# Four PSUM banks instead of two for the later pairs' scores and applications, in a newly found static order

## The chip, the cores and the metric

The kernel runs on one core of one Trainium2 chip. The metric is the time of one execution on the device in microseconds, the median of several runs. The engines are TensorE (PE in the rows), VectorE (DVE), ScalarE (ACT), GpSimd (POOL) and SyncE (SP, which issues the transfers). Each engine works through its own instructions in the order in which the program issues them.

## The reference

Three layers follow one another. The first is attention with 2 batches of 8 heads, 768 rows and 64 columns. Each row attends to the keys less than 16 rows away, and besides to one summary of each block of 32 rows: the maximum of its keys and the mean of its values.

```python
k_sum = k.reshape(B, H, nb, block, D).max(axis=3)
v_sum = v.reshape(B, H, nb, block, D).mean(axis=3)
scores_l = scale * np.matmul(q, k.transpose(0, 1, 3, 2))
scores_s = scale * np.einsum('bhsd,bhnd->bhsn', q, k_sum) + np.log(block)
scores_all = np.concatenate([np.where(mask_l, scores_l, -1e9), scores_s], axis=-1)
a = np.exp(scores_all - np.max(scores_all, axis=-1, keepdims=True))
x = np.matmul(a / (np.sum(a, axis=-1, keepdims=True) + 1e-09), np.concatenate([v, v_sum], axis=2))
```

The heads' outputs are joined to x, 1536 tokens of 512. The second layer divides x by its root mean square, multiplies it by a gain, and computes `silu(xn @ w_gate) * (xn @ w_val) @ w_out` with 1536 inner columns. The third computes `elu(x @ w_in) @ w_out` with 2048 inner columns.

## The kernel before

All three layers are fused and stay in the core's SBUF as far as they can. The 24 tiles of 64 query rows are handled as twelve pairs (b, j): batch b, pair j of 0 to 5. The 1536 tokens form three blocks of 512; the first block is made by the pairs (0,0) to (0,3). Matrix products are computed as three products of high and low parts of the operands (`THREE`), so each weight chunk and each x is split into a rounded copy (a cast, mostly ScalarE, L135) and the rest (a subtraction on VectorE, L146). The weights arrive in a packed form which `convert_a`, `convert_l` and `convert_b` turn into floats (L258 to L278) before the split.

For one pair `add_pair` lists these steps:

- `scores` (L495) writes 32 small matmuls into two PSUM banks, one for each half of the heads.
- `add_mask` on VectorE (L502) adds the mask and takes the maximum, `exps` on ScalarE (L513) takes the exponentials and their sums, and `normalize` divides (L528, L530, L533).
- `turn_e` (L538) transposes the weights on TensorE, one bank for each half; `copy_e` copies them out.
- `apply_v2` (L550) multiplies them with the values, one bank, and `copy_x2` copies the result to x, `xT`.

Around them stand `max_k` (L334, VectorE: the block maxima of the keys, `ksum`), `mean_v` (L370, TensorE: the sums of the values, `vp`), and for the first block the root mean square in two halves of 256 tokens: `square` and `add_square` (L635 to L641), `sum_square` (L648, TensorE, into a bank `pss`), `mean_square` (L653, VectorE), `root` (L659, POOL), `diagonal` (L672), `spread` (L686, TensorE), `keep_root`. `x_hi` and `x_lo` (L735, L744) split x times the gain.

The first feed-forward layer's products are `project` (L764): `pg` is a gate projection of one weight chunk, `pv_..c` the value projection, and the down products `acc` stand in L820. The blocks 1 and 2 later go through products of sums of quarter matrices (L1001, L1179).

PSUM has eight banks, each held by one tile at a time. A tile that takes a bank waits until its last holder's readers are done.

```python
MM, AT, ACC = ("m0", "m1"), ("t0", "t1"), ("a0", "a1", "a2", "a3")
BANKS = AT + MM + ACC[::-1]
```

The first four pairs may use all of `BANKS`; the eight later pairs, beside which the feed-forward layers already run, use `AT` for scores, transposes and applications, while the projections take `MM` and the down products `ACC`.

What sets the order is written out by hand as two tables. `PLAN` lists 2835 codes: a code divided by four is the operation's number, the rest is the choice among the engines that may do it. `TAGS` lists, digit by digit, which bank of its tuple a tile takes. The costs and due times in `add` are read by nothing while the kernel runs.

```python
for code in PLAN:
    i, choice = divmod(code, 4)
    engine, _, _, fn, args, _, _, new = self.ops[i]
    for tag, name in new:
        self.tag_of[name] = tag[int(next(picks))] if isinstance(tag, tuple) else tag
    fn(*((list(engine)[choice],) if isinstance(engine, dict) else ()), *args)
```

## Time and profile before

| | |
|---|---|
| median of 3 runs | 579.91 us (579.61 to 580.13) |
| profiled execution | 580.1 us, its span 578.4 us |
| granted clock of TensorE | 1.000 |
| busy: TensorE, VectorE, ScalarE, POOL | 571.3, 545.4, 428.3, 31.2 us |

The span goes from the first to the last instruction; what lies around it is 1.7 us here. Busy time of TensorE is that of its matmuls, whose ends are modelled, so rows of its timeline overlap: how long a step takes is read there from its start to the start of the next one. In a timeline, `x6` means six instructions of one form in a row, and a bracket at a row's end gives the idle time before it and what ended it.

### The profile page before, as it was taken

The page shows a single profiled execution, that of the slowest core. Times are in us where ns is not written, and L with a number is a line of the kernel's source. Part 1 is how long each engine was busy: PE and PEld are TensorE (multiplying, and loading weights), DVE is VectorE, ACT ScalarE, POOL GpSimd, SP SyncE. Part 2 cuts the span into 40 slices and gives each one's busy share as a digit, 9 for nine tenths or more (in the row PEclk, how much of TensorE's full clock was granted, in tenths as well). Part 3 has the DMA queues.
Part 4 walks back from the last instruction along what each step waited for, and adds up shares of the span by engine and source line. Part 5 has one row for each costly group of instructions (what it writes and reads, how often), then busy time and mean ns, then how long its engine had stood idle before and what let it go on. Part 6 is the DMA issues. An engine that isn't in the chain of part 4 may idle for free.

```text
span 578.4 us, 10028 instructions
## 1 busy us (share of the span) xinstructions
PE 571.3 (99%) x3369; PEld 467.6 (81%) x3369; DVE 545.4 (94%) x1155; ACT 428.3 (74%) x954; POOL 31.2 (5%) x73
## 2 busy tenths in 40 slices
PE   9899999999999999999999999999999999999997
PEld 5688787888878888888888888888888888888886
DVE  6999999999989999998799999999999999999992
ACT  5999997989999987643445557586577798879741
POOL 5630200000000000000000000000000000000000
PEclk9999999999999999999999999999999999999999
DMA  8999999889579994225251117242356527065112
GB/s 315 311 331 331 350 335 334 304 275 344 197 265 347 298 352 187 65 68 158 92 161 57 39 44 228 66 136 65 100 163 202 170 96 217 11 196 156 23 49 106
DMA packets 56181, 109.06 MB, mean 189 GB/s; under 512 B 6785, under 2 KB 19585, under 8 KB 56129
## 3 DMA queue, kind: packets, MB, share of 16 engines
q1 hardware_dynamic: 56128, 108.42, 56.6%
q8 instruction: 26, 0.43, 0.3%
q14 instruction: 27, 0.21, 0.1%
HBM read 80.09 MB, written 28.31 MB: 187 GB/s over the span
## 4 chain that ended last, share of the span: by engine, by line
PE 86%; DVE 9%; ACT 2%; issue 1%; DMA 1%; POOL 1%; SPq 0%; ACTq 0%; POOLq 0%
PE acc L820 12%; PE B_1u L1001 8%; PE ph L764 8%; PE A_1u L1001 6%; PE C_1u L1001 6%; PE B_2u L1001 6%; PE B_2d L1179 6%; PE B_1d L1179 4%; PE C_2d L1179 4%; PE C_2u L1001 4%; PE A_2u L1001 4%; PE A_2d L1179 4%; PE C_1d L1179 3%; PE A_1d L1179 3%; PE pg L764 2%; PE pv L550 2%
## 5 line engine op out<-in xcount | busy, mean ns | idle before, releaser
L1001 PE MATMUL B_1u<-xh,w_1u 128*128 128x512 f32 x144 | 48.4, 390 | 0.0
L764 PE MATMUL ph<-xa,ws_i 128*128 128x512 f32 x192 | 46.0, 392 | 0.0
L764 PEld LDWEIGHTS ph<-xa,ws_i 128*128 128x128 f32 x192 | 35.7, 188 | 7.6 <-issue 0.2
L764 PE MATMUL pg<-xs,ws_g 128*128 128x512 f32 (+1 forms) x168 | 36.4, 364 | 0.0
L1179 PE MATMUL B_2d<-td,wd 128*128 128x512 f32 x144 | 35.1, 389 | 0.0
L135 ACT CAST wd<-rd 128x512 fp32r<-128x512 f32 x49 | 29.7, 619 | 5.2 <-PE B_1d L1179 2.5
L146 DVE TENSOR_TENSOR wd<-rd,wd 128x512 fp32r<-128x512 f32 x49 | 32.7, 686 | 0.0
L1001 PE MATMUL C_1u<-xh,w_1u 128*128 128x512 f32 x96 | 32.6, 389 | 0.0
L1001 PE MATMUL B_2u<-xh,w_2u 128*128 128x512 f32 x96 | 32.6, 389 | 0.0
L1001 PE MATMUL A_1u<-xh,w_1u 128*128 128x512 f32 x96 | 32.5, 389 | 0.0
L1001 PEld LDWEIGHTS B_1u<-xh,w_1u 128*128 128x128 f32 x144 | 27.0, 188 | 6.0 <-ACT B_1u L135 0.3
L764 PEld LDWEIGHTS pg<-xs,ws_g 128*128 128x128 f32 x168 | 27.9, 189 | 4.6 <-issue 0.2
L1179 PEld LDWEIGHTS B_2d<-td,wd 128*128 128x128 f32 x144 | 27.0, 188 | 5.6
L1001 PE MATMUL B_1u<-xl,w_1u 128*128 128x512 f32 x72 | 28.0, 389 | 0.0
L135 ACT COPY h_1u<-B_1u 128x512 f32<-128x512 f32 x19 | 11.1, 590 | 22.6 <-PE B_1u L1001 19.7
L1179 PE MATMUL B_1d<-td,wd 128*128 128x512 f32 x108 | 26.5, 391 | 0.0
L1179 PE MATMUL C_2d<-td,wd 128*128 128x512 f32 x96 | 25.0, 389 | 0.0
L513 ACT ACTIVATE e<-e,nm 128x120 f32<-128x120 f32 x64 | 24.4, 387 | 0.0
L135 ACT CAST td<-z 128x512 fp32r<-128x512 f32 x28 | 17.1, 618 | 9.8 <-DVE z L1162 7.2
L1179 PEld LDWEIGHTS B_1d<-td,wd 128*128 128x128 f32 x108 | 20.2, 188 | 4.5 <-ACT B_1d L135 0.3
L1179 PE MATMUL A_2d<-td,wd 128*128 128x512 f32 x93 | 23.5, 389 | 0.0
L1001 PE MATMUL C_2u<-xh,w_2u 128*128 128x512 f32 x64 | 21.8, 389 | 0.0
(545 smaller groups left out, 1743.9 us busy)
## 6 DMA issues: line engine op xcount, KB each, us to landing
st_i<-in_moe_w_in SPq DMA_DIRECT2D x16, 512.0 KB, 5.7
st_p<-in_moe_w_out SPq DMA_DIRECT2D x16, 512.0 KB, 6.0
st_g<-in_moe_w_gate SPq DMA_DIRECT2D x12, 512.0 KB, 6.3
st_v<-in_moe_w_val SPq DMA_DIRECT2D x12, 512.0 KB, 5.9
st_o<-in_moe_w_out SPq DMA_DIRECT2D x12, 512.0 KB, 5.6
kept_i<-raw_i SPq DMA_DIRECT2D x16, 256.0 KB, 5.6
kept_p<-raw_p SPq DMA_DIRECT2D x16, 256.0 KB, 5.1
va<-in_v SPq DMA_DIRECT2D x17, 192.0 KB, 5.4
```

The source lines that it names most:

```text
L135: nc.scalar.copy(out=out, in_=in_)
L146: (nc.gpsimd if eng == POOL else nc.vector).tensor_sub(out, a, b)
L513: nc.scalar.activation(out=e[:, pr, :], in_=s[:, pr, :], func=AF.Exp, bias=nm[:, pr:pr + 1], scale=1.0 if pre else -1.0, accum_out=ss[:, p ...
L550: nc.tensor.matmul(pv[64 * h:64 * h + 64, pr, n, :], va[:NK, 2 * pr + h, :], T[f"ats{b}_{j}_{h}"][:, pr, QT * n:QT * n + QT], start=True, ...
L764: nc.tensor.matmul(pt[:, i], wt[:, a, kk * P:(kk + 1) * P], xt[:, c, i], start=(kk == 0 and n == 0), stop=(kk == KM - 1 and n == 2))
L820: nc.tensor.matmul(acc, wt[:, a, cs], ot[e], start=(first and n == 0), stop=(last and n == 2))
L1001: nc.tensor.matmul(pt, wt[:, a, cs], xt[e][:, kk], start=first and kk == n == 0, stop=kk == 1 and n == 2, skip_group_check=not first)
L1179: nc.tensor.matmul(pt, wt[:, a, cs], xt[:, e], start=first and n == 0, stop=last and n == 2, skip_group_check=i not in (0, 5))
```

## The change

Scores and applications of the eight later pairs may now use the banks of the projections too: `wide` is `AT + MM` for them, and a digit of `TAGS` chooses among four. Transposes stay in `AT`. Three costs in `add` are smaller. With these, the search that makes the two tables was run anew: the first 26 codes and the last 1363 of `PLAN` are the old ones, those between are another order. Every operation of the old table stands in the new one. Some 75 operations have another engine; in the lists of instructions ScalarE has 9 rows more than before, VectorE 5 and POOL 3 fewer. Lines behind L569 are one higher in the changed kernel.

```diff
     def add_pair(b, j, due, tags):
         i = b * NQ + 2 * j
         early = i < TPB
+        wide = tags if early else AT + MM
...
-            add(PE, 1.0, due + 0.5, scores, b, j, tags, pre, r=[f"q{b}_{j}"] + kas, w=[f"s{n}" for n in ns],
+            add(PE, 0.97, due + 0.5, scores, b, j, wide, pre, r=[f"q{b}_{j}"] + kas, w=[f"s{n}" for n in ns],
...
-                new=[x for n in ns if not pre for x in (("e", f"e{n}"), (tags, f"s{n}"))])
+                new=[x for n in ns if not pre for x in (("e", f"e{n}"), (wide, f"s{n}"))])
...
-            add(PE, 0.48, at + 5.2, turn_e, b, f"{j}_{h}", tags, r=[f"e{n}"], w=[f"at{n}"], new=[(tags, f"at{n}")])
+            add(PE, 0.465, at + 5.2, turn_e, b, f"{j}_{h}", tags, r=[f"e{n}"], w=[f"at{n}"], new=[(tags, f"at{n}")])
...
-        add(PE, 1.14, due + 6.9, apply_v2, b, j, tags, r=[f"ats{x}" for x in ns] + [x + y for x in bufs for y in ("#a", "#s")],
+        add(PE, 1.10, due + 6.9, apply_v2, b, j, wide, r=[f"ats{x}" for x in ns] + [x + y for x in bufs for y in ("#a", "#s")],
-            w=[f"pv{b}_{j}"], new=[(tags, f"pv{b}_{j}")])
+            w=[f"pv{b}_{j}"], new=[(wide, f"pv{b}_{j}")])
...
-    40, 48, 52, 80, 320, 64, 60, 212, 226, 84, 229, 218, 108, 232, 236, 92, 584, 112, 96, 336, 480, 120, 340, 326,
+    20, 40, 48, 52, 80, 320, 64, 60, 212, 226, 84, 229, 218, 108, 232, 236, 92, 584, 112, 96, 336, 480, 120, 340, 326,
...
-    "2551001014507341614711001241075617267054601543015125100101101010001101010010110001010011010011010101"
+    "2551001014507341614711001241075617267056314250320115010010111021011000231010101221001110110030010120"
```

On TensorE the first 37 and the last 300 operations are in their old order (from 24.9 to about 305 us they differ), on VectorE the first 35 and the last 480. What stands at three places follows, as lists of instructions without times; a name ends in the tile's number, and `x3` stands for three in a row.

VectorE, before, where the first pairs end (`ats` are transposed weights copied out, `rs` a reciprocal, `raw_v` and `raw_g` weight chunks being converted):

```order
L137 COPY xT_171<-pv_0_541 128x4x128
L523 RECIPROCAL rs_3_0_587<-ss_3_0_563 128x4
L137 COPY ats_2_1_632<-at_2_1_591 120x512
L523 RECIPROCAL rs_3_1_634<-ss_3_1_569 128x4
L269 TENSOR_SCALAR raw_v_662<-st_v_583 128x512
L530 TENSOR_TENSOR e_3_1_568<-e_3_1_568,rs_3_1_634 128x480
L278 SCALAR_TENSOR_TENSOR raw_v_662<-st_v_583,raw_v_662 128x512
L274 SCALAR_TENSOR_TENSOR raw_g_667<-st_g_581 128x512
L641 TENSOR_TENSOR 0, 1)slice(0, 256, None)_676<-0, 1)slice(0, 256, None)_676,2, 3)slice(0, 256, None)_678 128x512
```

And of the change:

```order
L334 TENSOR_REDUCE ksum_197<-kT_1_580 128x4x4
L137 COPY ats_1_0_583<-at_1_0_533 120x512
L137 COPY xT_171<-pv_0_542 128x4x128
L523 RECIPROCAL rs_3_0_591<-ss_3_0_564 128x4
L523 RECIPROCAL rs_3_1_645<-ss_3_1_570 128x4
L137 COPY ats_2_1_647<-at_2_1_596 120x512
L269 TENSOR_SCALAR raw_v_652<-st_v_587 128x512
L530 TENSOR_TENSOR e_3_1_569<-e_3_1_569,rs_3_1_645 128x480
L274 SCALAR_TENSOR_TENSOR raw_g_607<-st_g_585 128x512
L334 TENSOR_REDUCE ksum_197<-kT_2_626 128x4x4
L278 SCALAR_TENSOR_TENSOR raw_v_652<-st_v_587,raw_v_652 128x512
L642 TENSOR_TENSOR 0, 1)slice(0, 256, None)_633<-0, 1)slice(0, 256, None)_633,2, 3)slice(0, 256, None)_631 128x512
```

Two block maxima of the second batch (`ksum_197`, from `kT_1` and `kT_2`) now stand here. Before, they stand some 50 rows further down or more.

VectorE, before, where the first products' operands are made (`xs_0` to `xs_3` are the parts of x, `ws_v` and `ws_g` weight chunks; `ws_g_760` is gate chunk 0, `ws_g_766` gate chunk 2):

```order
L744 SCALAR_TENSOR_TENSOR xs_3_721<-xT_171,g_sb,xs_3_721 128x256
L274 SCALAR_TENSOR_TENSOR raw_g_730<-st_g_598 128x512
L744 SCALAR_TENSOR_TENSOR xs_2_719<-xT_171,g_sb,xs_2_719 128x256
L146 TENSOR_TENSOR ws_v_754<-raw_v_662,ws_v_754 128x512
L744 SCALAR_TENSOR_TENSOR xs_1_758<-xT_171,g_sb,xs_1_758 128x256
L744 SCALAR_TENSOR_TENSOR xs_0_717<-xT_171,g_sb,xs_0_717 128x256
L146 TENSOR_TENSOR ws_g_760<-raw_g_667,ws_g_760 128x512
L146 TENSOR_TENSOR ws_g_766<-raw_g_730,ws_g_766 128x512
```

And of the change, where `ws_g_756` is chunk 0 and `ws_g_814` is chunk 2:

```order
L146 TENSOR_TENSOR ws_g_756<-raw_g_607,ws_g_756 128x512
L274 SCALAR_TENSOR_TENSOR raw_g_784<-st_g_603 128x512
L143 TENSOR_SCALAR xs_0_683<-xT_171,g_sb 128x256
L143 TENSOR_SCALAR xs_3_687<-xT_171,g_sb 128x256
L745 SCALAR_TENSOR_TENSOR xs_0_683<-xT_171,g_sb,xs_0_683 128x256
L745 SCALAR_TENSOR_TENSOR xs_1_738<-xT_171,g_sb,xs_1_738 128x256
L745 SCALAR_TENSOR_TENSOR xs_2_685<-xT_171,g_sb,xs_2_685 128x256
L745 SCALAR_TENSOR_TENSOR xs_3_687<-xT_171,g_sb,xs_3_687 128x256
L638 TENSOR_TENSOR  1)slice(256, 512, None)_867<-xT_171 128x512
L146 TENSOR_TENSOR ws_g_814<-raw_g_784,ws_g_814 128x512
```

Between the splits of chunks 0 and 2 there are now the conversion of chunk 2, two `x_hi`, the second half's four `x_lo` and a square.

TensorE, before, at the first products (`pss` is the first half's sum of squares, `s_5` the scores of pair (0,5), `pv_3` an application):

```order
L648 MATMUL pss0slice(0, 256, None)_710<-ones,0, 1)slice(0, 256, None)_676 128x4 x4
L495 MATMUL s_5_0_732<-ka_10_379,q_5_600 64x120
...
L550 MATMUL pv_3_771<-ats_3_0_752,va_168 64x64
...
L764 MATMUL pv_0c<-xs_0_717,ws_v_754 128x256 x3
...
L764 MATMUL pg_0_816<-xs_0_717,ws_g_760 128x256 x3
...
L764 MATMUL pg_2_854<-xs_0_717,ws_g_766 128x512 x3
L764 MATMUL pg_2_854<-xs_1_758,ws_g_766 128x512 x3
L648 MATMUL ss0slice(256, 512, None)_861<-ones, 1)slice(256, 512, None)_839 128x4 x4
```

And of the change:

```order
L649 MATMUL pss0slice(0, 256, None)_742<-ones,0, 1)slice(0, 256, None)_633 128x4 x4
L550 MATMUL pv_3_759<-ats_3_0_754,va_168 64x64
...
L495 MATMUL s_5_0_788<-ka_10_380,q_5_605 64x120
...
L765 MATMUL pv_0c<-xs_0_683,ws_v_740 128x256 x3
...
L765 MATMUL pg_0_842<-xs_0_683,ws_g_756 128x256 x3
...
L765 MATMUL pg_0_842<-xs_0_683,ws_g_756 128x256 x3
...
L765 MATMUL pg_2_888<-xs_0_683,ws_g_814 128x512 x3
L765 MATMUL pg_2_888<-xs_1_738,ws_g_814 128x512 x3
L649 MATMUL ss0slice(256, 512, None)_895<-ones, 1)slice(256, 512, None)_867 128x4 x4
```

The scores of (0,5) have moved behind application (0,3), and gate chunk 0 is finished in both halves (`pg_0_842` twice four instructions) ahead of chunk 2.

TensorE, before, at the scores of pair (1,0) (`s_0_0` and `s_0_1`) and the application of (0,4) (`pv_4_1316`):

```order
L764 MATMUL pv_4c<-xs_1_758,ws_v_1136 128x512 x3
L495 MATMUL s_0_0_1248<-ka_0_1227,q_0_1166 64x120
L495 MATMUL s_0_1_1249<-ka_0_1227,q_0_1166 64x120
...
L764 MATMUL pv_4c<-xs_2_719,ws_v_1136 128x512 x3
L764 MATMUL pv_4c<-xs_3_721,ws_v_1136 128x512 x3
L820 MATMUL acc_0_0_1286<-act_0_0h,ws_o_1174 128x512
...
L550 MATMUL pv_4_1316<-ats_4_0_1235,va_170 64x64
L550 MATMUL pv_4_1316<-ats_4_1_1162,va_170 64x64
```

And of the change:

```order
L765 MATMUL pv_4c<-xs_3_687,ws_v_1117 128x512 x3
L495 MATMUL s_0_0_1269<-ka_0_1239,q_0_970 64x120
L495 MATMUL s_0_1_1270<-ka_0_1239,q_0_970 64x120
...
L495 MATMUL s_0_1_1270<-ka_1_1166,q_0_970 64x120
L550 MATMUL pv_4_1289<-ats_4_0_1252,va_170 64x64
L550 MATMUL pv_4_1289<-ats_4_1_1248,va_170 64x64
...
L550 MATMUL pv_4_1289<-ats_4_1_1248,va_230 64x64
L765 MATMUL pg_6_1337<-xs_0_683,ws_g_1100 128x512 x3
```

Six matmuls of a value projection and six of the down products stood between the two steps; now the application is right behind the scores.

## Rows read from the trace of the kernel before

**Rows 1.** The page: busy time of each engine, share of the span, instructions.

```profile
PE 571.3 (99%) x3369; PEld 467.6 (81%) x3369; DVE 545.4 (94%) x1155; ACT 428.3 (74%) x954; POOL 31.2 (5%) x73
```

**Rows 2.** The list of TensorE's waits: us in total, times, longest us.

```profile
PE at L538 <- POOL e L528: 1.4, 2, 0.7
```

**Rows 3.** Windows, the stretch from 22 to 57 us: busy time of each engine.

```profile
22.00:57.00 35.00, 34.32 (x388) 30.09 (x386) 34.38 (x99) 34.49 (x93) 10.78 (x15) 1.00 0.93 314
```

**Rows 4.** TensorE's timeline, 127 to 138 us: start, us, what, count [idle before].

```profile
127.20 1.52 PE L764 MATMUL pv_10c<-xs,ws_v 128*128 128x512 f32 x6
128.65 1.05 PE L495 MATMUL s<-ka,q 64*64 64x120 f32 x32
129.63 1.67 PE L764 MATMUL pv_10c<-xs,ws_v 128*128 128x512 f32 x6
131.14 0.39 PE L820 MATMUL acc<-act_7h,ws_o 128*128 128x512 f32 x1
...
135.24 1.52 PE L764 MATMUL pg<-xs,ws_g 128*128 128x512 f32 x6
136.60 1.52 PE L764 MATMUL pv_11c<-xs,ws_v 128*128 128x512 f32 x6
```

**Rows 5.** TensorE's timeline, an application between products.

```profile
149.88 1.15 PE L550 MATMUL pv<-ats,va 120*64 120x64 f32 x32
150.96 0.50 PE L820 MATMUL acc<-act_11h,ws_o 128*128 128x512 f32 x1
151.29 0.39 PE L820 MATMUL acc<-act_11l,ws_o 128*128 128x512 f32 x1
```

**Rows 6.** TensorE's timeline, transposes and an application, 94 to 100 us.

```profile
94.23 0.60 PE L538 MATMUL at<-ident,e 128*120 128x128 f32 x4
94.58 1.63 PE L764 MATMUL pv_7c<-xs,ws_v 128*128 128x512 f32 x6
96.06 0.60 PE L538 MATMUL at<-ident,e 128*120 128x128 f32 x4
96.58 1.15 PE L550 MATMUL pv<-ats,va 120*64 120x64 f32 x32
...
98.93 0.40 PE L820 MATMUL acc<-act_3h,ws_o 128*128 128x512 f32 x1
99.52 0.65 PE L538 MATMUL at<-ident,e 128*120 128x128 f32 x4 [0.19 <-DVE xT L137]
```

**Rows 7.** TensorE's timeline, the early stretch.

```profile
29.43 1.16 PE L495 MATMUL s<-ka,q 64*64 64x120 f32 x32 [0.28 <-PE 0slice(0, 256, None)_710 L648]
30.52 0.92 PE L550 MATMUL pv<-ats,va 120*64 120x64 f32 x24
...
32.10 1.69 PE L764 MATMUL pv_0c<-xs,ws_v 128*128 128x256 f32 x12
...
36.45 1.04 PE L648 MATMUL lice(256, 512, None)_861<-ones,lice(256, 512, None)_839 128*128 128x4 f32 x8
...
42.37 1.75 PE L764 MATMUL pg<-xs,ws_g 128*128 128x512 f32 x6
```

**Rows 8.** VectorE's timeline, the same stretch.

```profile
29.25 0.47 DVE L744 SCALAR_TENSOR_TENSOR xs<-xT,g_sb,xs 128x256 fp32r<-128x256 f32 x1
...
33.25 0.27 DVE L502 CUSTOM_DVE_ANT_0 e<-s,mask 128x120 f32<-128x120 f32 x1
...
34.13 1.66 DVE L744 SCALAR_TENSOR_TENSOR xs<-xT,g_sb,xs 128x256 fp32r<-128x256 f32 x4
35.71 0.68 DVE L641 TENSOR_TENSOR lice(256, 512, None)_839<-lice(256, 512, None)_839,lice(256, 512, None)_835 128x512 f32<-128x512 f32 x1
36.31 0.67 DVE L334 TENSOR_REDUCE ksum<-kT 128x16 f32<-128x512 f32 x1
```

**Rows 9.** POOL's timeline, the two roots of the first block.

```profile
34.28 0.90 POOL L659 TENSOR_TENSOR 0slice(0, 256, None)_841<-0slice(0, 256, None)_810,mhalf 128x2 f32<-128x2 f32 x1 [0.16 <-DVE 0slice(0, 256, None)_810 L653]
38.86 2.04 POOL L659 TENSOR_TENSOR lice(256, 512, None)_894<-lice(256, 512, None)_885,mhalf 128x2 f32<-128x2 f32 x1 [3.67 <-DVE lice(256, 512, None)_885 L653]
```

More of the change, by code (lines that the diff above doesn't have):

```diff
@@ L1353 @@
     392, 152, 357, 296, 301, 264, 396, 176, 156, 164, 172, 180, 360, 592, 365, 185, 520, 116, 268, 124, 492, 497, 525,
[146 rows of a table removed]
[146 rows of a table added]
 )
 TAGS = (
-    "2551001014507341614711001241075617267054601543015125100101101010001101010010110001010011010011010101"
-    "0010101010110100100110110012222011032111012200416700322510242117120215102402217620102321100604512120"
+    "2551001014507341614711001241075617267056314250320115010010111021011000231010101221001110110030010120"
+    "0110101010110100101101100100011122003122001012560004230721420200110701251412217620102321100604512120"
     "1212631050101032047120100112140022625222010213122640172000115222002600010530111047231562102072202130"
```

292 rows, old and new, of the table PLAN are left out of this document.

## The prediction

> **What bounds the kernel now.** I read the page first. TensorE is busy 571.3 us of a span of 578.4 [rows 1], at the full granted clock, so the time is close to the sum of the matmuls, which the change leaves as they are. Only three things can move: time in which TensorE waits, time lost where it goes from one kind of matmul to another, and new waits.
>
> The list of TensorE's waits comes next [rows 2]. It holds very little, 3.4 us in six rows: its largest is 1.4 us for POOL's normalization of the first pairs, ahead of 24.9 us, where the order on TensorE stays as it is, and of the others only waits of 0.2 to 0.3 each lie where the order changes [rows 6, 7]. The windows then say which engines have no room while the attention and the first feed-forward block run side by side: from 22 to 57 us VectorE is busy 34.38 of 35 us and ScalarE 34.49 [rows 3]. There, whatever is put ahead of an urgent instruction on these two engines makes that one later by about its own length. Behind 57 us there is more room on both, and TensorE has only one short wait there that the change touches.
>
> Last I read TensorE's timeline from start to start, because the ends of its matmuls are modelled and the rows overlap.
>
> **Joins.** Six products alone take 1.36 us (135.24 to 136.60). The six ahead of a scores step take 1.45 (127.20 to 128.65), the scores 0.98 (128.65 to 129.63), the six behind them 1.51 (129.63 to 131.14) [rows 4]. Going into scores so costs 0.09 and going back to products 0.15. An application takes 1.08 (149.88 to 150.96), and the one product behind it 0.33 where one alone takes 0.23 (a sixth of 1.36), so its way back costs 0.10 [rows 5]; its way in I take as that of scores, 0.09.
>
> With four banks to choose from, later scores can now stand right beside an application: scores of pair (1,0) and application (0,4), application (0,5) and scores (1,1), application (1,1) and scores (1,2). None of the old order's later steps has such a join. Each saves one way back and one way in. Scores first: 0.15 + 0.09 = 0.24, less what going from scores to an application costs. One early row shows at most 0.11 for that: the scores at 29.43 last 1.09 until the application at 30.52, against 0.98 [rows 7]. Application first: 0.10 + 0.09 = 0.19, less a change that no row shows, 0 to 0.11. I take the row's 0.11 for the first join, which leaves 0.13, and nothing for the change of the other two, since no row shows one: 0.13 + 2 x 0.19 = 0.51. The bounds are 0.13 + 2 x 0.08 = 0.29 and 0.24 + 2 x 0.19 = 0.62. The Trainium skill, page TensorEngine Tiling (Array Packing), section Key Properties, says that a change of tiling mode, not merely of the tile, drains TensorE. Scores stand in the trace as 64*64 and applications as 120*64, so by that page a join would still hold one drain of the four; as an estimate from it the three joins would give 3 x 0.43 / 4 = 0.32 (0.43 is the sum of the four costs above), and the forecast would be 0.2 us higher. The early row at 29.43 agrees with it, with its 0.11, and is a single one.
>
> Transposes of the weights (`turn_e`) have four joins more than before. A row of that kind exists: a transpose at 96.06, then an application at 96.58, 0.52 together with the change. Alone the transpose takes 0.35 (94.23 to 94.58), its way back 0.12 (the six products from 94.58 to 96.06 take 1.48), and the way into an application 0.09: 0.56 [rows 6]. The gain is 0.04 a join, and I cost it at nothing.
>
> **The wait at 99.** The product at 98.93 is followed by the next transpose only at 99.52, 0.59 instead of 0.23 [rows 6]: the transpose (1,1,0) goes into the bank t0 that application (1,0) holds until it is copied out. In the changed order that application goes into m0, and both transposes stand ahead of it. The 0.36 goes.
>
> **The gate projection at 42.** Six products from 42.37 last 1.75 where 1.52 is usual [rows 4, 7]; this is 0.2 of waiting for the split of weight chunk 3. The changed order puts the value sums (24 short matmuls) ahead of it, which hide it: 0.2 gained.
>
> **The early stretch.** Here VectorE's order matters, and it is the largest term. Three edits are behind it. Two block maxima of the second batch (`max_k`) stood at 36.31 and at 44.63 and now stand before the first masks of pair (0,4); a row of 0.67 or 0.68 takes 0.60 from start to start (35.71 to 36.31), so everything behind them comes 1.2 later [rows 8]. The sums of squares of the first half go to bank t0, which the scores of pair (0,5) need next, so these wait for `mean_square` on VectorE. And the split of gate chunk 2 moves behind the second half's x work, while TensorE now asks for it after 24 half products of chunk 0 instead of 12.
>
> First the scores: the masks of (0,4) end at about 29.3 in the trace; 1.2 for the maxima, 0.6 for the split of the value chunk and 0.4 for one `x_lo` (a quarter of 34.13 to 35.71) give 31.45, `mean_square` 0.07 more. The scores start at 31.5, last 0.98, and the first products start at 32.5 instead of 32.10 [rows 7, 8]: 0.38 lost.
>
> Then chunk 2: its split ends by 33.25 now. Ahead of it come the two maxima 1.2, four `x_lo` 1.58, one square 0.6, and two `x_hi` on VectorE, which the trace doesn't have at this width; the nearest row is an `x_lo` of the same shape at 0.40, and a plain scaling with one input less can't be far under half of that, so 0.3 each, bounds 0.2 and 0.4. The sum is 3.98, and the split ends at 37.23 [rows 8]. TensorE is there after the same amount of work as from 32.10 to 36.45, so at 32.48 + 4.35 = 36.83 [rows 7]. It waits 0.4. The lag behind the old order is 37.23 - 36.45 = 0.78, which holds the 0.38. Bounds: nothing, if one of the two inputs comes earlier by another engine's work, and 1.2, if the maxima's full price reaches TensorE. Other moved work (about 75 operations change their engine, some 5 us more for ScalarE) lies from 57 us on beside products that don't wait for it; I cost it at nothing, and a few tenths if that cover fails.
>
> One load is moved: the second batch's keys (512 KB) go to SP's queue ahead of the first gate weights. Behind it on that queue are four loads that the first products need. No wait of TensorE is put down to a load in the list of waits, so these have room, and I cost the move at nothing; what it costs if the room is too small is one more delay of the first products, inside the bounds of the lag above.
>
> The sum is -0.51 - 0.36 - 0.2 + 0.78 = -0.3, and a tenth or two for a spread of the second half that comes late (below): -0.15. The profiled execution took 580.1 us, 0.2 over the median of the runs, 579.91, so the forecast is 579.8 on the median's scale.
>
> **Rivals.** A measurement of this kernel can tell about 0.2%, 1.16 us, from no change; that is the band of "same", 578.75 to 581.07.
>
> *Nothing is lost early.* If VectorE has more room than its busy time says, the early lag isn't there, and with it goes the 0.28 that the scores waited at 29.43 [rows 7]. Then -0.51 - 0.36 - 0.2 - 0.3 = -1.4, about 578.5; with the upper price for the joins and 0.04 for each of the transposes' four, 578.3. For it: the three old waits there are short and each has another cause. Against: the three edits on VectorE add up in rows, and nothing in them is free. Chance 0.27.
>
> *ScalarE stands behind the root.* The second half's `diagonal` moves from VectorE to ScalarE, and stands there ahead of the casts of gate chunk 3 and value chunk 1. Its input comes from POOL's power, which took 0.90 us once and 2.04 the other time [rows 9]. The second sums of squares come 2.2 later than now (37.23 + 1.42 for the chunk's first half, 38.65 against 36.45 [rows 7]); with the root 2.4 behind them as now (38.86), it starts at 41.1 and ends at 42.0 or at 43.1. If ScalarE is at the diagonal when the root starts, it stands idle for the root's length, in a stretch where it has 0.5 us of room in 35 [rows 3], and VectorE's splits behind its casts, then TensorE, get what is over. It decides when ScalarE stands there for more than about a us, half of which its room and TensorE's lag of 0.8 take up; the price is 1.2 to 2.0 on top of the sum, the upper end being a whole slow root, 581 to 581.8. The Trainium skill, page SBUF — State Buffer, section on two separate sides, says that VectorE and GpSimd share one pair of ports as an exclusive lock and that the loser fully blocks; a busy VectorE would by that make the slow root the usual one. The two rows of the root agree with that no more than with chance. The slower outcome has 0.21.
>
> *The change doesn't do what it says.* If a join costs as much as two separate entries, only the waits at 42 and 99 are gained: -0.56 + 0.78 + 0.15 = +0.4, 580.3. This lies in the same band.
>
> **How the numbers follow.** The likeliest case, with the last rival, is no measurable change: 0.52, at 579.8, its own range 579.1 (joins at 0.62, a lag of 0.4) to 580.9 (joins at 0.29, a lag of 1.2, the late spread and half a us of lost cover). Faster has 0.27 and slower 0.21 from the two others. The range takes in most of both: 578.2, just under the end of the first, to 581.8, the end of the second.
>
> **What would show it.** In the new trace: the three joins start to start (an application right behind scores at 1.0 to 1.1 us); no gap ahead of the transposes of (1,1); the first products near 32.5 and a gap of 0.4 ahead of gate chunk 2 near 37; ScalarE's idle time ahead of `diagonal`, with POOL as the releaser. The prediction is wrong if TensorE is ahead of its old self at equal work at 45 us, or more than 1.5 us behind it, or if new gaps of over half a us come up between 57 and 240 us.

## The result, and the profile after

The changed kernel took 587.15 us (median of 5 runs, 586.22 to 587.6); the kernel before took 580.13 beside it (579.61 to 581.15). The ratio is 1.0113, 95% interval 1.0102 to 1.0125: slower by 1.1%, outside the range of the prediction. The profiled execution took 586.43 us, its span 584.7, at a mean granted clock of 0.993. All five runs of the changed kernel lie at 0.993 or 0.994; the profiled execution of before has 1.000.

The page's busy times after, which answer to [rows 1]:

```profile
PE 573.8 (98%) x3369; PEld 470.8 (81%) x3369; DVE 544.5 (93%) x1148; ACT 432.9 (74%) x967; POOL 28.2 (5%) x70
```

The same matmuls, 2.5 us more of busy time, and 3.8 us more in which TensorE isn't busy (10.9 of 584.7 against 7.1 of 578.4). The list of TensorE's waits after, beside [rows 2]:

```profile
PE s L495 <- POOL ka L450: 2.7, 1, 2.7
PE at L538 <- POOL e L528: 1.4, 2, 0.7
...
PE pv L550 <- DVE ats L137: 0.8, 2, 0.6
PE pv L550 <- DMA va<-in_v: 0.5, 1, 0.5
PE pv L550 <- ACT ats L135: 0.3, 1, 0.3
```

The first row is new and is the largest: scores wait 2.7 us for POOL to fill a part of a key tile, `ka`. The windows show where, beside [rows 3] (start and end; busy us and instructions of PE, PEld, DVE, ACT, POOL; granted clock, DMA share, GB/s):

```profile
22.00:32.00 10.00, 8.56 (x166) 6.93 (x164) 9.96 (x33) 9.97 (x29) 6.39 (x8) 1.00 0.97 280
32.00:42.00 10.00, 7.32 (x67) 6.72 (x63) 8.77 (x29) 9.15 (x28) 2.87 (x3) 0.66 0.86 334
42.00:57.00 15.00, 15.00 (x137) 13.33 (x136) 11.26 (x28) 9.96 (x26) 0.99 (x2) 1.00 0.65 210
```

From 32 to 42 us TensorE is busy 7.32 us and its clock is granted at 0.66 of full speed: it stands still, and then it runs slowly. Behind 42 the other engines have room that they didn't have before. TensorE's timeline after, beside [rows 7]:

```profile
24.37 1.15 PE L550 MATMUL pv<-ats,va 120*64 120x64 f32 x32 [0.59 <-DVE ats L137]
...
28.37 1.15 PE L550 MATMUL pv<-ats,va 120*64 120x64 f32 x32 [0.26 <-ACT ats L135]
29.62 1.05 PE L649 MATMUL 0slice(0, 256, None)_742<-ones,)slice(0, 256, None)_633 128*128 128x4 f32 x8
31.12 1.15 PE L550 MATMUL pv<-ats,va 120*64 120x64 f32 x32 [0.45 <-DMA va<-in_v]
32.21 0.52 PE L495 MATMUL s<-ka,q 64*64 64x120 f32 x4
35.40 1.86 PE L495 MATMUL s<-ka,q 64*64 64x120 f32 x28 [2.68 <-POOL ka L450]
37.20 2.93 PE L765 MATMUL pv_0c<-xs,ws_v 128*128 128x256 f32 x12
39.92 4.96 PE L765 MATMUL pg<-xs,ws_g 128*128 128x256 f32 x30
44.72 0.95 PE L649 MATMUL lice(256, 512, None)_895<-ones,lice(256, 512, None)_867 128*128 128x4 f32 x8
45.53 1.69 PE L765 MATMUL pv_0c<-xs,ws_v 128*128 128x256 f32 x12
47.05 0.60 PE L687 MATMUL 0slice(0, 256, None)_941<-0slice(0, 256, None)_871,ones 128*128 128x256 f32 x2
```

The scores of pair (0,5) start at 32.21, 0.7 us later than forecast; the execution had lost 0.73 us by 7 us already (below). Four of their 32 matmuls run, and the 28 others stand until 35.40. Then the price of the clock shows: those 28 take 1.80 us (35.40 to 37.20) where 28/32 of the usual 0.98 is 0.86; twelve half products take 2.72 (37.20 to 39.92) and twelve of the same form 1.52 further on (45.53 to 47.05). Taken by single microseconds, the granted clock is 1.00 up to 34 us, 0.50 (the level of 1.2 GHz) from 35 to 41, and 1.00 again from 42.

POOL's timeline tells why `ka` came late:

```profile
26.94 2.89 POOL L736 TENSOR_SCALAR xs<-xT,g_sb 128x256 fp32r<-128x256 f32 x3 [0.81 <-DMA g_sb<-in_moe_rms_g]
32.39 0.52 POOL L428 MEMSET va<- 32x512 f32 x1 [2.56 <-PE pv L550]
32.99 2.24 POOL L660 TENSOR_TENSOR 0slice(0, 256, None)_777<-0slice(0, 256, None)_749,mhalf 128x2 f32<-128x2 f32 x1
35.20 0.15 POOL L450 MEMSET ka<- 128x64 f32 x1
46.02 0.75 POOL L660 TENSOR_TENSOR lice(256, 512, None)_905<-lice(256, 512, None)_900,mhalf 128x2 f32<-128x2 f32 x1 [10.67 <-DVE lice(256, 512, None)_900 L654]
```

A fill of 0.15 us, on which the scores of (0,5) depend, stands behind two instructions: the fill of a value tile, which waits 2.56 us for application (0,3) to be done with that tile, and the first half's root, 2.24 us. In the old order the same fill of `ka` stands ahead of both, and is done at 28.60; POOL's row before:

```profile
28.45 0.15 POOL L450 MEMSET ka<- 128x64 f32 x1
```

From here on **lag** is the start of a TensorE operation after less the start of the same one before, taken where both orders have done the same set of operations. It is 0.73 us at 7 us, 1.53 at the first sums of squares (29.62 against 28.09), 5.10 at the first products (37.20 against 32.10), 7.02 at 49.39 against 42.37, 6.75 at 68.53 against 61.77, 5.66 at 107.16 against 101.50, and 5.83 at the last product. So some 7 us are lost ahead of 50 us, and 1.1 are won back between 62 and 101, where the banks are used:

```profile
71.36 1.05 PE L495 MATMUL s<-ka,q 64*64 64x120 f32 x32
72.35 1.15 PE L550 MATMUL pv<-ats,va 120*64 120x64 f32 x32
73.53 1.85 PE L765 MATMUL pg<-xs,ws_g 128*128 128x512 f32 x7
...
88.37 1.15 PE L550 MATMUL pv<-ats,va 120*64 120x64 f32 x32
89.45 1.05 PE L495 MATMUL s<-ka,q 64*64 64x120 f32 x32
90.44 0.50 PE L821 MATMUL acc<-act_2h,ws_o 128*128 128x512 f32 x1
...
105.12 1.03 PE L538 MATMUL at<-ident,e 128*120 128x128 f32 x8
106.08 1.15 PE L550 MATMUL pv<-ats,va 120*64 120x64 f32 x32
```

Scores ahead of an application take 0.99 and the application 1.18 with its way back (1.08 + 0.10); the application at 88.37 takes 1.08 and the scores behind it 0.99. Going from the one to the other costs nothing in these rows. The transposes of (1,1) at 105.12 run in one piece; the wait of [rows 6] is gone.

### The profile page after: what moved, and what is told of

The parts are those of the page before. It is cut to its first block, busy times and chain, and to the rows that moved or that the text cites. A ratio compares the mean times of both kernels' runs of the same rounds, so it can differ in the third digit from the quotient of the medians.

```text
span 584.7 us, 10043 instructions
## 1 busy us (share of the span) xinstructions
PE 573.8 (98%) x3369; PEld 470.8 (81%) x3369; DVE 544.5 (93%) x1148; ACT 432.9 (74%) x967; POOL 28.2 (5%) x70
## 4 chain that ended last, share of the span: by engine, by line
PE 95%; DVE 1%; POOL 1%; DMA 1%; ACT 1%; issue 0%; SPq 0%; ACTq 0%; POOLq 0%
PE acc L821 13%; PE B_1u L1002 8%; PE ph L765 8%; PE pg L765 6%; PE B_2u L1002 6%; PE B_2d L1180 6%; PE C_1u L1002 6%; PE A_1u L1002 6%; PE B_1d L1180 4%; PE C_2d L1180 4%; PE C_2u L1002 4%; PE A_2u L1002 4%; PE A_2d L1180 4%; PE C_1d L1180 3%; PE A_1d L1180 3%; PE pv L550 2%
## 5 line engine op out<-in xcount | busy, mean ns | idle before, releaser
L765 PE MATMUL ph<-xa,ws_i 128*128 128x512 f32 x192 | 47.5, 394 | 0.0
L1002 PE MATMUL A_2u<-xh,w_2u 128*128 128x512 f32 x64 | 21.7, 389 | 0.0
```

The lines of the kernel that those rows point to most:

```text
L765: nc.tensor.matmul(pt[:, i], wt[:, a, kk * P:(kk + 1) * P], xt[:, c, i], start=(kk == 0 and n == 0), stop=(kk == KM - 1 and n == 2))
L1002: nc.tensor.matmul(pt, wt[:, a, cs], xt[e][:, kk], start=first and kk == n == 0, stop=kk == 1 and n == 2, skip_group_check=not first)
```

## The experiments

Theory: POOL's order makes the pause, the pause makes the slow clock, and the banks do what was forecast. Rival, from the prediction: VectorE's and ScalarE's order (the two `max_k`, the diagonal behind the root) cost most, and the fill only shows it. In the table, each ratio is to the kernel before as it ran beside that kernel, at a median of 580.12 to 580.63.

| kernel | median us (runs) | ratio, 95% |
|---|---|---|
| e1_keys_first | 583.42 (7) | 1.0044, 1.0028 to 1.0060 |
| e2_warm | 587.06 (6) | 1.0112, 1.0091 to 1.0134 |
| e3_old_early | 586.81 (4) | 1.0112, 1.0099 to 1.0125 |
| e4_new_early | 588.40 (4) | 1.0149, 1.0134 to 1.0164 |
| e5_old_52 | 584.25 (6) | 1.0058, 1.0043 to 1.0073 |
| e6_old_46 | 580.72 (11) | 1.0012, 1.0001 to 1.0022 |
| e7_kmax_late | 584.63 (6) | 1.0065, 1.0045 to 1.0086 |
| e8_kload_late | 583.17 (12) | 1.0037, 1.0020 to 1.0055 |
| e9_elu_first | 580.78 (11) | 1.0003, 0.9994 to 1.0012 |
| e10_one_bank | 580.33 (11) | 1.0002, 0.9994 to 1.0011 |
| e11_warm_elu | 585.69 (4) | 1.0097, 1.0083 to 1.0112 |
| e12_keys_mid | 584.73 (6) | 1.0076, 1.0051 to 1.0102 |
| e13_store1 | 580.26 (12) | 1.0006, 0.9994 to 1.0019 |
| e14_store2 | 580.94 (11) | 1.0015, 1.0006 to 1.0023 |
| e15_after2 | 585.81 (6) | 1.0085, 1.0061 to 1.0108 |

**One code moved** (805 is the fill of `ka`, 796 that of the value tile, 432 the root):

```diff
-648, 796, 432, 805, 548,
+648, 805, 796, 432, 548,
```

> The changed kernel with one code moved in PLAN: the key copy of the last tile of batch 0, whose zero fill runs on POOL, stands ahead of the zero fill of a value tile and of the first root on POOL instead of behind both. Theory: POOL's queue alone held the scores of (0,5) for 2.68 us, and TensorE's clock fell to its lower level because of that pause, for another 2.6 us. Both go: about 581.9 us (587.15 - 5.3), granted clock 1.00 throughout. Rival one, the clock falls for another reason in this stretch: only the pause goes, about 584.5. Rival two, the next wait takes over (the split of gate chunk 2 on VectorE, at 37.9 us), so that 1 to 2 us of the gain are lost again: 583 to 584 with the clock at 1.00.

It took back 3.7 of the 7.0 us, less than the 5.3 expected. POOL fills `ka` at 29.25 and the scores don't wait. But the next thing shows; TensorE's timeline of this kernel:

```profile
27.87 1.15 PE L550 MATMUL pv<-ats,va 120*64 120x64 f32 x32 [1.03 <-DMA va<-in_v]
...
31.31 1.97 PE L550 MATMUL pv<-ats,va 120*64 120x64 f32 x32 [1.30 <-DVE xs L745]
```

Two applications wait 1.0 and 1.3 us, the clock falls again for a shorter time, and the lag is 2.83 at the first products.

**Idle matmuls in the pause.** The change, with 14 matmuls on `idle_w` ahead of the scores of (0,5):

```diff
     def scores(...):
+        if (b, j) == (0, 5):
+            pt = bank_of("a0")
+            for _ in range(14):
+                nc.tensor.matmul(pt, idle_w, ..., start=True, stop=True)
```

> The changed kernel with its order as it is, and 14 extra matmuls on an idle bank right ahead of the scores of (0,5); they add work and no result uses them. They fill the pause without shortening it (14 x 0.216 us = 3.0 us). Theory: the clock fell because TensorE stood still, so it stays at 1.00 and about 2.6 us come back: 584.5 us. Rival: the clock falls in this stretch whatever TensorE does, or the pause costs nothing by the clock: 587.2 us.

TensorE's timeline, then its window:

```profile
32.07 3.19 PE L491 MATMUL warm_s<-idle_w 128*128 128x512 bf16 x14
35.19 1.05 PE L499 MATMUL s<-ka,q 64*64 64x120 f32 x32
36.17 1.69 PE L769 MATMUL pv_0c<-xs,ws_v 128*128 128x256 f32 x12
...
165.96 7.36 PE L769 MATMUL ph<-xa,ws_i 128*128 128x512 f32 x24 [1.92 <-DVE ex L806]
```

```profile
32.00:42.00 10.00, 10.00 (x95) 7.67 (x90) 8.57 (x28) 9.00 (x28) 2.82 (x3) 1.00 0.86 338
```

The scores wait just as long, but the clock stays at 1.00, and the lag at 46.6 us is 4.26 instead of 7.02. So the pause made the clock fall, and the fall cost as much as the pause. By its median the time isn't better for it: at 165.96 a new wait of 1.92 us brings the clock down again (the mean from 140 to 180 us is 0.96). One of the six executions kept 1.000 throughout; it took 583.32, where 584.5 was expected.

**The seam moved.** Four kernels take the first codes from one order and what is left from the other:

```diff
-PLAN = after
+PLAN = before[:360] + rest_of(after)   # e3; 257 in e5, 221 in e6
+PLAN = after[:320] + rest_of(before)   # e4
```

> The order of before for its first 360 codes (TensorE's first 70 operations, to about 63 us), and the changed order and banks for all that is left. Theory: the whole loss is in the early stretch and the later order with its joins and its missing wait gains about 1.2 us: 579.0 us. Rival: the later order gains nothing, or a new wait arises at the seam: 580.1 us or more.

> The complement: the changed order for its first 320 codes (to about 62 us) and the order of before for what is left, its scores and applications in the two old banks. Theory: all of the loss and none of the gain, about 588.3 us. Rival, the loss is spread over the later stretch: below 586 us.

By their times both are inconclusive: each has a pause at its own seam, the place where one order hands over to the other (3.77 us ahead of scores at 69.53 in the first, 2.73 us at value chunk 3, at 64.74, in the second). That e4 comes out at its 588.3 is luck: behind the changed early stretch its lag is 3.70 and not 7.02, and the pause at its seam makes up for that. Up to its seam e3 lags by 0.99, of which 0.73 is its start. The early stretch of e4 has the codes of the changed kernel, but its scores waited 1.07 for `ka`, where the change's waited 2.68. POOL's row and TensorE's in e4:

```profile
32.21 0.82 POOL L660 TENSOR_TENSOR 0slice(0, 256, None)_777<-0slice(0, 256, None)_749,mhalf 128x2 f32<-128x2 f32 x1
```

```profile
33.19 1.86 PE L495 MATMUL s<-ka,q 64*64 64x120 f32 x28 [1.07 <-POOL ka L450]
```

The root takes 0.82 here and 2.24 in the changed kernel. So about 1.4 of the 2.68 is the length of this root, and that differs between executions of the same codes. The clock fell here too, to 0.50, but for some three us (33 to 36, and 0.79 from 36 to 37).

> The order of before for its first 257 codes (TensorE's first 52 operations, to about 42 us), the changed order and banks for the rest; at this seam the two orders have done nearly the same work. Theory one: all of the loss is early (the pause at the scores of (0,5) and what it makes late), and the later order gains 1.1 us by joins and a missing wait: 579.0 us, two or three tenths more for the seam. Theory two: the changed order asks for the third layer's weights earlier than the transfers can bring them, whatever happens early; then the scores of (1,4) are followed by a wait for the first products' ELU near 160 us and the time is 581 us or more. Rival: a new pause early in the later order, with the clock: 585 us or more.

> The same with the seam earlier: the order of before for its first 221 codes (TensorE's first 46 operations, to about 36 us), which hold the scores of (0,5) and the fill ahead of the roots. Theory one: 579.0 us, or up to 0.8 more if the later place of gate chunk 2's split and the diagonal on ScalarE cost what was predicted. Theory two: 581 us or more, by the wait near 160 us.

The seam of e5 again has a wait of 2.7 us, the rival that was named for it. That of e6, behind 46 TensorE operations (about 35 us), has none: with the old order up to there the whole loss is gone, and at 100 us TensorE is 1.43 us ahead of before, 0.42 of it from its start. It doesn't stay ahead. TensorE's timeline of e6, and ScalarE's:

```profile
159.44 1.05 PE L495 MATMUL s<-ka,q 64*64 64x120 f32 x32
161.91 5.73 PE L765 MATMUL ph<-xa,ws_i 128*128 128x512 f32 x24 [1.41 <-DVE ex L802]
```

```profile
157.05 0.68 ACT L258 ACTIVATE st_i<-st_i 128x512 f32<-128x512 f32 x1 [0.83 <-DMA st_i<-in_moe_w_in]
...
158.78 0.69 ACT L258 ACTIVATE st_p<-st_p 128x512 f32<-128x512 f32 x1 [0.55 <-DMA st_p<-in_moe_w_out]
159.36 0.62 ACT L135 CAST xh<-xT 128x512 fp32r<-128x512 f32 x1
159.87 0.60 ACT L796 ACTIVATE ex<-ph 128x512 f32<-128x512 f32 x1
```

The exponential of the ELU (L796) stands behind conversions of weights that have only just landed; the product at 161.91 needs the bank that the ELU reads. A TensorE that comes earlier meets loads that don't come earlier.

**The loads of the early stretch.** e7 is e1 with `max_k` (1,2) and (1,5) put back behind the masks; e8 is e7 with two key loads put back; e12 has POOL's three in the order value fill, key fill, root.

```diff
 e7: -500, 940, 944, 373,        +500, 940, 373,
     -1644, 1712, 960, 1772,     +1644, 1712, 1772,
     -681, 3280, 956,            +681, 3280, 944, 960, 956,
 e12: -648, 796, 432, 805, 548,  +648, 796, 805, 432, 548,
```

> The changed kernel with the key copy ahead on POOL (as e1_keys_first), and two of the second batch's block maxima moved back on VectorE, to just ahead of the third. Theory: the maxima cost the application (0,1) 0.59 us, that makes two loads of values later, and these make the applications (0,2) and (0,3) wait for 1.0 and 1.3 us and the clock fall for 3 us. All of it goes: 580.5 us, no pause over half a us between 22 and 37 us. Rival: the loads of values are late because 512 KB of keys stand ahead of them in SP's queue, not because of the maxima: 583 us, with only the 0.6 gained.

> As e7_kmax_late, and the two early loads of the second batch's keys (512 KB each) behind the first block's weights and values again, as before. Rival of the run before: the waits of the applications (0,2) and (0,3) go only here, 1 us or more below e7_kmax_late. Theory: no difference beyond 0.3 us.

> The changed kernel with the key copy's fill on POOL between the fill of the value tile and the first root. Theory: of the pause of 2.7 us the fill of the value tile makes 0.8 (it waits for the application (0,3)), and the root the rest; the pause is 0.6 to 0.8 us, the clock stays up, and the time is near that of e1_keys_first, 583.4 us. Rival: the fill of the value tile alone makes the pause long enough for the clock to fall: 585.5 us or more.

The executions of all three, and of e1, differ by what the clock does. Where it stays at 1.000 throughout they take 580.82 and 581.06 (e1, two runs of seven), 581.06 (e7, one of six), 579.84 to 580.69 (e8, four of twelve; a fifth took 583.46) and 581.74 (e12, one of six); at a lower mean they take 582.36 to 588. One execution of e15 (below), which has the changed kernel's order on TensorE, also kept 1.000, at 582.38: there too the pause or the fall behind it isn't the same each time, and which of the two was missing isn't shown. The profiled runs have the lower clock, with waits of applications for value tiles of 3.0 and 1.2 us in e7, for a value tile and for VectorE of 1.07 and 1.23 in e12, and for ScalarE's copy and VectorE of 0.87 and 0.86 in e8. So e7 misses its 580.5 by its median and by its waits. In e7 the wait of 0.59 at application (0,1) is gone, as expected of `max_k`. The scores of e12 wait only 0.30 for `ka`, so the fill of the value tile alone makes little of the pause; the two waits ahead of it bring the clock down.

The loads of the first two value tiles from 20 us on (two loads, KB each, median us from issue to landing), in e7 and in e8:

```profile
va<-in_v SPq DMA_DIRECT2D x2, 192.0 KB, 5.3
```

```profile
va<-in_v SPq DMA_DIRECT2D x2, 192.0 KB, 3.1
```

This goes through all profiles: the eight with the key loads ahead (the changed kernel, e1, e2, e4, e7, e11, e12, e15) have 4.2 to 5.8 us for each of these two loads, the nine others 2.4 to 3.7. So the moved key loads do delay them. What that costs in time stays open: e7 and e8 differ by less than either spreads, and in the changed kernel both have landed by 27.61, ahead of application (0,2).

**Out of the late wait.** e9 is e6 with one conversion (`convert_a` of the third layer's output weights, 2496) behind the ELU on ScalarE, e11 is e2 with the same move, e10 is before with application (1,0) in bank m0.

```diff
 e9, e11: -1400, 2496, 2572,   +1400, 2572,
          -4044, 4048, 4052,   +4044, 4048, 2496, 4052,
 e10 (TAGS): -01011000101      +01011200101
```

> As e6_old_46, and near 158 us one conversion of a weight chunk of the third layer moved on ScalarE from ahead of the first products' ELU to behind it; the conversion waits for its transfer. Theory: the 1.4 us that TensorE waits for the ELU there come from ScalarE standing in front of transfers that are late by what the new order asks, and not from the ELU's own work; the wait goes and the time is 579.3 us. Rival: the transfers are the bound of this whole stretch, and the wait only moves to the next products behind the moved chunk: 580.7 us as before.

> As e2_warm (14 idle matmuls fill the pause at the scores of (0,5); they add work that no result uses), with the same move on ScalarE as in e9_elu_first. Theory: what the kept clock gave back early in e2_warm was lost again in front of the ELU near 160 us; with that wait gone the 2.6 us stay: 584.5 us. Rival: everything behind is late by the transfers, whichever instruction meets it first: 587 us.

> The order of before, code for code, with one digit of TAGS changed: the application (1,0) takes the bank m0 instead of t0, so that the next transpose no longer waits for its copy. Theory: 0.36 us go at 99 us and stay gone, 580.07 against 580.43, which a trace shows and the times hardly do. Rival: the wait comes back within 60 us as another one, and TensorE ends where it ended.

In e9 the product that had waited at 161.91 starts at 160.66, straight behind the scores; e11 is 1.4 us faster than e2 by the medians, with intervals that overlap. In e10 the wait at 99 is gone, but the application at 97.48 now waits 0.54 for the SiLU on VectorE. Neither e9 nor e10 can be told from before.

**The end.** In all changed kernels but e8, e10 and e13 the end behind the last products is longer: 4.87 us from the last row of TensorE to the span's end after (579.83 to 584.7), 4.86 in e9 (573.64 to 578.5), 4.40 before (574.00 to 578.4). SyncE's last two issues are what differs; e13 and e14 issue one or two of the last stores as halves, which puts instructions into SyncE's program, and e15 is the changed kernel with two.

```diff
-        nc.sync.dma_start(out=out[rows, n * TB:(n + 1) * TB], in_=T[src])
+        for lo, hi in ((0, TB // 2), (TB // 2, TB)) if (a, n) in HALVED else ((0, TB),):
+            nc.sync.dma_start(out=out[rows, n * TB + lo:n * TB + hi], in_=T[src][:, lo:hi])
```

> This is the last kernel (first 46 TensorE operations as before, later order as changed, one conversion behind the ELU) with one of the late stores of the output issued as two halves, which puts one instruction more into SyncE's program. In the profiles the end behind the last products took 4.40 us before (574.00 to 578.4) and 4.86 in the last kernel (573.64 to 578.5): SyncE stands still for 0.3 us at one place of its program, which lies between the last two issues there and moves back by one instruction for each instruction more. Theory (the pause sits at a fixed place of the program): one instruction more puts it ahead of the wait for the last copies, where SyncE waits anyway; the end takes 4.4 us, and the time falls by 0.45 against the last kernel, 580.3 by its median, or 579.5 to 580 if the gain of the banks (1.2 us at equal work) arrives whole. Rival (the longer end belongs to the later order, by the state of the queues): the end stays at 4.86 and the time at 580.8.

> The same with two of the late stores as halves, two instructions more. Theory: the pause falls one instruction earlier still, which is also hidden behind a wait; end 4.4 us, time as with one store. Rival: end 4.86, time 580.8.

> The changed kernel with two late stores as halves, which brings SyncE's program to the length of the kernel before. Theory: the end takes 4.4 us instead of 4.87, the time falls by 0.45 to 586.7. Rival: 4.87 and 587.15. The early pause of TensorE is untouched in both.

SyncE's last row before, in e9 and in e13 (two issues in each):

```profile
575.35 0.81 SPq L835 DMA_DIRECT2D out<-ob  x2
```

```profile
574.99 1.08 SPq L836 DMA_DIRECT2D out<-ob  x2
```

```profile
577.73 0.81 SPq L837 DMA_DIRECT2D out<-ob  x2
```

The pause between the two issues goes in all three kernels (0.81, 0.82, 0.83), so it sits at a place of SyncE's program: counted through the traces, SyncE stands still for 0.34 to 0.43 us behind its 591st instruction in all kernels but before, e10 and e13, where it waits at that place anyway. In e8, whose program is a little shorter, the place lies behind the last issue; its pair takes 0.81 and its end 4.37. Of these three, the end gets shorter in e13 alone: 4.52 (576.38 to 580.9), against 4.99 (574.41 to 579.4) in e14 and 4.86 in e15, where SyncE then waits 1.6 us for the stores to land. So the place was right, and the shorter end fails in two of three; some 0.3 us hang on it. e13's 580.26 is the 580.3 expected, but against before it is no nearer than e9.

## Why the prediction was wrong

**The early stretch, +0.78 forecast, some +7 measured: the step that failed.** The prediction followed VectorE's order and the PSUM bank to the scores of (0,5), put them at 31.5, and they began at 32.21, which is the 0.73 of the start. That part of the path was right, and so was VectorE's sum for chunk 2: its split was done at 37.88, 37.15 without the start, where 37.23 had been forecast. TensorE asked for it only at 43.33, so the forecast wait of 0.4 could not show. What failed is the path to the scores: the prediction never asked what else they read. Their key tile is filled on POOL, and POOL's order had been turned round there; POOL's queue and TensorE's clock stand in no term of the sum, and the two cost 5.35 us. The loss up to 49 us adds up from rows: 0.73 at the start, which is run to run (below); 0.59 and 0.26 for weights copied late; 0.45 for a value load; 2.68 for the pause; and 2.67 for the clock, which is 0.94 at the scores and 1.20 at the twelve half products (above), and 0.53 at the first twelve of the gate's (1.97, 39.92 to 41.89, for 1.44). Less the two waits of 0.28 that the old order had, this is 6.8 of 7.02. e1 and e2 show the pause's cause and the clock's; that the old first 46 operations give the time of before within 0.2% (e6) leaves nothing of that size behind them. That the pause was 2.68 and not nearer to 1 is the slow root's part (e4), which differs between executions.

The two `max_k` did cost on VectorE, as priced, but elsewhere: 0.59 at application (0,1), and e7 takes it away. The prediction counted one moved key load and put it at nothing, for the loads behind had room. Two stand earlier (issued at 10.90 and 17.03 us, before at 14.87 and 30.74), and they do delay value loads, as the rows of e7 and e8 show; whether any of the 7 us is theirs stays open.

**ScalarE behind the root**, the rival of the slower side, happened: ScalarE's row of the second diagonal reads

```profile
46.80 0.69 ACT L671 ACTIVATE lice(256, 512, None)_919<-ident,lice(256, 512, None)_905 128x128 f32<-128x128 f32 x2 [5.65 <-POOL lice(256, 512, None)_905 L660]
```

It stands idle 5.65 us there, more than feared, but because TensorE's second sums of squares are themselves 6 us late, and no wait of TensorE follows. Where TensorE is less late the idle time is 0.66 (e1) and 0.94 (e8), where it is on time (e6, e9, e14) there is none, and in none of these profiles does TensorE wait between 40 and 57 us. So the chance of 0.21 for slower went to a mechanism that cost nothing here.

On the root itself I was half wrong. I had cited the Trainium skill, page SBUF — State Buffer, section on two separate sides, and taken from it that a busy VectorE makes the slow root the usual one. The Trainium skill ties the lock there to certain VectorE instructions (those in a 2-port mode, and those with two inputs in SBUF beside a GpSimd instruction that reads it), a condition that I had left out. In the profiles VectorE is busy all through nearly every root of the first block, and most take 0.75 to 0.90. The slow ones come back at the same places: the first root of the changed order takes 2.24, 2.19 (e2) and 2.26 (e15), but 1.35 in e11 and 0.82 in e4; the second root of the old order takes 2.03 or 2.04 in all four profiles that keep it. That points to what runs beside the root; that it is the lock isn't shown.

**The joins and the wait at 99 were right, by their sum.** Forecast were 0.51 and 0.36; the lag falls by 1.09 from 62 to 101 us after, by 1.10 in e1 and 1.09 in e2. Taken between products well inside a projection, it goes from 6.67 (62.32 us before) to 6.35 (90.35) and to 5.62 (108.50). The first 0.32 holds the first two joins, 0.24 + 0.19 by their rows; 24 gate products behind the first of them take 5.70 us (73.53 to 79.23) where 5.44 is usual, which uses up a part. The other 0.73 holds the wait (0.36) and the third join (0.19); up to 0.16 of the rest may be the transposes' joins, which I had priced at nothing. The 0.11 that I took from one early row for a change between scores and application isn't in the later rows. The rule of the Trainium skill, page TensorEngine Tiling (Array Packing), section Key Properties, by which a change of mode drains the engine, would have left one drain in each join; at 64*64 beside 120*64 the rows show no price for it, and the measurement decides.

**The gate projection at 42** can't be read for itself; the lag falls by 0.27 between 42 and 62 us, where 0.2 was forecast.

**Why the gain isn't in the time either.** In e6, e9 and e13 the big loss ahead of 46 operations is gone. The lag still falls by 1.2 from 42 to 101 us in e6 and e9 and by 0.6 in e13, and yet these kernels run level with before. In e10, which has only the other bank, it rises by 0.2 (0.28 to 0.48): the wait of 0.36 goes, and the new one of 0.54 outweighs it. Part comes back as waits for the other engines: 1.41 at 161.91 and 0.33 at 128.97 in e6; in e13

```profile
94.28 0.65 PE L538 MATMUL at<-ident,e 128*120 128x128 f32 x4 [0.27 <-ACT xT L135]
...
104.42 1.15 PE L550 MATMUL pv<-ats,va 120*64 120x64 f32 x32 [0.34 <-ACT ws_g L135]
...
131.62 3.02 PE L765 MATMUL pg<-xs,ws_g 128*128 128x512 f32 x12 [0.52 <-DVE th L793]
```

and up to 0.46 at the end. The changed kernel, 6 us late, shows none of these waits between 57 and 160 us. That is argued from single profiles. In e9's the gain even stays to the end: its lag is 0.60 at 7 us, by its start, and -0.36 at the last product; the start and the longer end hide it. Over its eleven runs e9 is still not faster, and what the other executions lose stays open. No version ran measurably faster than before.

## What to carry to other kernels

When an order changes, follow every operand of the instruction that waits next, through every queue, a 0.15 us fill on a nearly idle engine too: what stands ahead of it in that queue, and what that waits for. A pause of TensorE is priced with the clock that follows it, read from a window behind the pause. And a gain on the bounding engine may come back as waits for the engines and loads behind it, which come no earlier (e6).

## What the runs showed of the hardware

- One pause of 2.68 us, with other work on TensorE ahead of it and waits of 0.59 and less, was followed by six us at 1.2 GHz, which cost 2.67 us more; with TensorE kept busy (e2) nothing of that was lost. The length of the slow stretch doesn't follow that of the pause: behind 2.67 us in e5 (0.50 from 46 to 48 us, 0.52 and 0.78 in the us on either side) and 1.07 us in e4 it lasted some three us.
- The same root on POOL, in the same codes, took 2.24, 2.19, 2.26, 1.35 and 0.82 us in five profiles, with VectorE busy all through.
- Two 192 KB loads took 4.2 to 5.8 us from issue to landing with two loads of 512 KB moved ahead in SyncE's queue, and 2.4 to 3.7 without.
- The start varies from run to run: the same first matmuls put TensorE between 0.57 us ahead of before and 0.74 behind it at 5 to 8 us; the 23 runs of before in one set lie 1.7 us apart (579.61 to 581.30).
- SyncE loses 0.3 us behind the 591st instruction of its program in these kernels: where that lies between the last two issues, the pair takes 1.06 to 1.10 us and not 0.81 to 0.83.
